# A banded attention with a gated MLP on one core: the same steps in another written-out order, on other PSUM banks

## The chip, the cores and the metric

One core of one Trainium2 chip runs the whole program. The metric is the time on the device in microseconds. The kernel before was run three times without a profile and once with one; every trace row below comes from the profiled run.

## The reference, cut to what matters

The input has 8 batches, 8 heads, 576 positions and a head size of 64. Heads 0 to 3 attend to the last 32 positions, heads 4 to 7 to the earlier positions that agree modulo 32. The heads' results side by side are `x` (8 x 576 tokens, 512 wide), and a gated MLP with a convolution over three neighbouring tokens follows.

```python
scores = np.where(masks, q @ k.T / sqrt(64), -1e9)
x = softmax(scores) @ v
h = np.maximum(x @ w_in, 0.0)                        # 512 -> 1024
conv_out = sum(conv_w[k] * h_shifted[k] for k in range(3))
out = (h * sigmoid(conv_out)) @ w_out                # 1024 -> 512
```

## The kernel before, in words

**Attention** works in 32 units, one for each batch and pair of heads. A unit loads q and k together (`load_qk`, L218) and v (`load_v`, L223) into one of two buffers, unit n into buffer n mod 2. TensorE makes the scores (L369, with masks at L376) in one half of the PSUM tile `r`. DVE and ACT make the softmax, and DVE transposes it into `tt` (L447). TensorE then makes the values from `tt` and v (L470). From unit 4 on, the values of unit n and the scores of unit n + 1 are one step, a "visit". ACT copies the values as rounded `xh` (L503), DVE takes the rest as `xl` (L528). So the load of q for unit n + 2 waits for the scores of unit n, and the load of v for unit n + 2 for the values of unit n.

**Weights** arrive as 64-bit floats in blocks of 512 KB (L245), and DVE, ACT, POOL (clamp, L281) and TensorE split each into a high and a low part, the `w_in` blocks first and then the `w_out` blocks (`convert`).

**The MLP** takes the 4608 tokens in 9 groups of 512. For each group `mm1` makes 8 blocks of 128 hidden channels: per block four product steps of three matmuls each (high by high, low by high, high by low; L567), gathered in one of four PSUM banks `m0` to `m3`. `conv_gate` then works on one block: ACT evicts it with relu (L580), ACT scales it (L592; DVE at L595 for some blocks of the first group), DVE adds the two neighbours (L601), ACT takes tanh (L604), DVE the gate (L605), ACT and POOL split the result into `gh` and `gl` (L608, L610). POOL also carries two tokens from group to group (L582, L584). `mm2` makes the 4 output blocks of a group, eight product steps each (L633), ACT evicts a block (L640) and SyncE stores it (L643).

The blocks in flight live in the tile `misc`: three buffers `h` and three buffers `c`, used in turn. `mm2` evicts its output blocks into the same buffers: three of the four into `c` buffers, which the next group's scale writes, and one into an `h` buffer, which the next relu writes. A later block can take such a buffer only when the store that reads it has landed.

**The order** is written out by hand. Each `op(...)` call appends one step with its engine, what it reads and what it writes, and gives it the next number (0 to 2148). `ORDER` (L42) lists all numbers, and the program is emitted in that order. Each engine has one queue and works through its steps in the order in which they were emitted. SyncE issues all 120 DMAs, loads and stores alike, in that way: a DMA whose buffer isn't free holds all that stand behind it. `BANKS` (L39) names the PSUM bank of each of the 128 accumulations. `FILLS` (L126) puts dummy products on a tile of zeros ahead of a step: a bank, a number of wide ones (512 columns) and of narrow ones (256).

```python
    def emit(self, busy):
        for i in ORDER:
            bank, wide, narrow = FILLS.get(i, (0, 0, 0))
            for j in range(wide + narrow):
                busy(bank, j < wide)
            self.ops[i][2]()
```

Steps that are named below:
- 30, 56, 69: the values of units 0, 2 and 3; 10, 22, 35, 48, 61: the scores of units 0 to 4; 317: the visit with unit 6's scores.
- 59 and 60: the loads of q and of v for unit 4; 47: the load of v for unit 3; 130 and 131: the last two blocks of `w_in`; 170 and 169: the first two blocks of `w_out`.
- 58: the `xl` of unit 2, which the scores of unit 4 need; 171: the clamp of the first `w_out` blocks, on DVE.
- 82, 92, 106, 115, 126, 128: TensorE's part in the splitting of `w_in` blocks.
- 1531, 1541, 1551, 1561: the four stores of group 5; 1699: the load of v for unit 29; 1569: the first scale that takes a buffer of step 1531.

Of the kernel before, what the change touches and what calls it, by code (L numbers as in the profile page):

```python
# [39 lines left out]
    "10321030203132021200031230013102313220230203213000233002203113020221123003211032002110233022132012030212233123121130032131002321"  # L40
)
ORDER = [  # L42
# [82 lines left out]
]  # L125
FILLS = {  # L126
    22: (0, 6, 1), 30: (0, 17, 1), 35: (1, 5, 1), 43: (0, 1, 1), 128: (0, 1, 1), 10: (0, 11, 0), 56: (4, 5, 0), 185: (4, 4, 1), 219: (2, 3, 0),
}

class Plan:  # L130
# [636 lines left out]
```

## Time and profile before

| What | us |
|---|---|
| median of 3 runs (lowest, highest) | 520.11 (519.94, 521.47) |
| the profiled execution's own time | 523.03 |
| its span in the profile | 521.0 |
| TensorE busy | 497.7 |
| DVE busy | 367.4 |
| ACT busy | 282.1 |
| POOL busy | 133.7 |

The span runs from the first to the last instruction of the profiled execution; its own time holds 2.0 us more around that. Busy time counts matmuls, loads of weights apart from them, and the work of the other engines; waiting and issuing of DMAs are not busy. Starts are counted from the beginning of the span. A wait is put down to what released it last.

### The profile page before, as it was taken

Reading aid. Unit: us, or ns where it says so; the run is one execution under the profiler, and the core shown is the slowest. Engines: PE = TensorE matmul, PEld = TensorE weight load, DVE = VectorE, ACT = ScalarE, POOL = GpSimd, SP = SyncE. Lnnn points to the kernel's source line nnn. Section 1 sums busy time; section 2 is a strip of 40 time slices with the busy share of each in tenths; the row PEclk is TensorE's granted clock in tenths of the full one; section 3 lists DMA queues with packets and bytes.
Section 4 is the critical chain, followed back from the end, with each engine's and each line's share of the span. In section 5 each row is a group of like instructions: output and inputs, shape, how many; then the busy total and the mean of one; then the engine's idle time right before and its main releaser. Section 6 shows DMA issues by size and latency. Waiting matters only on the chain.

```text
span 521.0 us, 15912 instructions
## 1 busy us (share of the span) xinstructions
PE 497.7 (96%) x6936; PEld 399.4 (77%) x6936; DVE 367.4 (71%) x655; ACT 282.1 (54%) x611; POOL 133.7 (26%) x216
## 2 busy tenths in 40 slices
PE   8778999999999999999998999999989999999997
PEld 4456768788888778878876888788768888878897
DVE  3996999786956797378767985798548855753640
ACT  4883687367624663257435743674347534755551
POOL 0200253023411251025302440233005220542240
PEclk9997999999999999999999999999989999999999
DMA  8583334432232304440252213422431202001001
GB/s 313 229 292 104 109 107 143 174 132 81 79 115 83 119 3 143 111 140 9 70 171 68 95 67 102 140 71 79 119 119 33 78 3 82 0 1 60 23 11 71
DMA packets 17349, 51.42 MB, mean 99 GB/s; under 512 B 2048, under 2 KB 2944, under 8 KB 17280
## 3 DMA queue, kind: packets, MB, share of 16 engines
q1 hardware_dynamic: 17280, 50.41, 28.5%
q8 instruction: 54, 0.88, 0.7%
q14 instruction: 15, 0.12, 0.1%
HBM read 40.97 MB, written 9.44 MB: 97 GB/s over the span
## 4 chain that ended last, share of the span: by engine, by line
PE 69%; DMA 6%; DVE 5%; ACT 4%; issue 1%; SPq 1%; ACTq 0%
PE m L633 37%; PE m L567 23%; DMA out_dram<-misc 6%; PE r L470 5%; PE r L369 3%; DVE misc L601 3%; ACT misc L592 1%; ACT misc L580 1%; DVE misc L605 1%; SPq L218 1%; DVE tt L447 1%; ACT misc L604 1%; ACT gh L608 1%; SPq L643 0%; ACT xh L503 0%
## 5 line engine op out<-in xcount | busy, mean ns | idle before, releaser
L601 DVE SCALAR_TENSOR_TENSOR misc<-misc,cw 128x512 f32<-128x512 f32 (+23 forms) x256 | 130.4, 548 | 48.2 <-ACT misc L592 46.6
L567 PE MATMUL m<-xh,wih 128*128 128x512 f32 x288 | 116.8, 406 | 4.3 <-ACT misc L580 4.3
L633 PE MATMUL m<-gh,woh 128*128 128x512 f32 (+2 forms) x320 | 119.5, 373 | 1.2 <-ACT misc L580 1.2
L633 PE MATMUL m<-gl,woh 128*128 128x512 f32 (+2 forms) x320 | 117.9, 369 | 0.0
L633 PE MATMUL m<-gh,wol 128*128 128x512 f32 (+2 forms) x320 | 117.8, 368 | 0.0
L610 POOL TENSOR_TENSOR gl<-misc,gh 128x512 fp32r<-128x512 f32 (+1 forms) x70 | 88.1, 1265 | 112.9 <-ACT gh L608 112.4
L567 PE MATMUL m<-xh,wil 128*128 128x512 f32 x288 | 113.9, 395 | 0.0
L567 PE MATMUL m<-xl,wih 128*128 128x512 f32 x288 | 113.7, 395 | 0.0
L592 ACT ACTIVATE misc<-misc,cw 128x255 f32<-128x255 f32 (+15 forms) x122 | 59.3, 523 | 22.6 <-DMA out_dram<-misc 12.3
L567 PEld LDWEIGHTS m<-xh,wih 128*128 128x128 f32 x288 | 55.1, 191 | 18.6 <-ACT misc L580 6.9
L633 PEld LDWEIGHTS m<-gh,woh 128*128 128x128 f32 x320 | 60.1, 188 | 12.0 <-ACT misc L580 1.7
L633 PEld LDWEIGHTS m<-gl,woh 128*128 128x128 f32 x320 | 60.1, 188 | 10.5 <-POOL gl L610 0.2
L604 ACT ACTIVATE misc<-misc 128x512 f32<-128x512 f32 (+1 forms) x72 | 44.8, 630 | 42.7 <-DVE misc L601 42.4
L633 PEld LDWEIGHTS m<-gh,wol 128*128 128x128 f32 x320 | 60.1, 188 | 9.7
L567 PEld LDWEIGHTS m<-xl,wih 128*128 128x128 f32 x288 | 55.1, 191 | 12.1
L567 PEld LDWEIGHTS m<-xh,wil 128*128 128x128 f32 x288 | 55.3, 192 | 10.8
L582 POOL COPY misc<-carry 128x2 f32<-128x2 f32 x64 | 21.3, 341 | 160.6 <-DMA out_dram<-misc 83.1
L580 ACT ACTIVATE misc<-m 128x512 f32<-128x512 f32 x72 | 42.7, 593 | 30.4 <-PE m L567 15.3
L605 DVE SCALAR_TENSOR_TENSOR misc<-misc 128x512 f32<-128x512 f32 (+1 forms) x72 | 51.0, 717 | 9.9 <-ACT misc L604 9.4
L608 ACT CAST gh<-misc 128x512 fp32r<-128x512 f32 (+1 forms) x72 | 43.9, 616 | 20.9 <-DVE misc L605 20.4
L640 ACT ACTIVATE misc<-m 128x512 f32<-128x512 f32 (+2 forms) x40 | 21.8, 558 | 46.1 <-PE m L633 45.9
L503 ACT CAST xh<-r 128x576 fp32r<-128x576 f32 (+13 forms) x56 | 23.8, 429 | 40.3 <-PE r L470 37.0
(76 smaller groups left out, 490.3 us busy)
## 6 DMA issues: line engine op xcount, KB each, us to landing
qk<-in_dram SPq DMA_DIRECT2D x32, 592.0 KB, 5.4
v<-in_dram SPq DMA_DIRECT2D x32, 384.0 KB, 4.0
ws<-in_dram SPq DMA_DIRECT2D x14, 512.0 KB, 4.8
out_dram<-misc SPq DMA_DIRECT2D x28, 256.0 KB, 4.1
misc<-in_dram SPq DMA_DIRECT2D x2, 512.0 KB, 8.4
out_dram<-misc SPq DMA_DIRECT2D x4, 255.5 KB, 2.8
out_dram<-misc SPq DMA_DIRECT2D x3, 256.5 KB, 2.1
more<-in_dram SPq DMA_DIRECT2D x1, 320.0 KB, 5.7
```

The costliest lines, as they stand in the source:

```text
L470: nc.tensor.matmul(psV[64 * h:64 * h + 64, o:o + n_], v[W * c:W * c + W, h, j], tt[W * c:W * c + W, 64 * NBLK * h + a:64 * NBLK * h + z], ...
L503: op(A, "xh", lambda hi=hi, src=src: nc.scalar.copy(hi, src), ko, [("xh", hp, x) for x in halves], n=z - a)
L567: nc.tensor.matmul(ps, a[:, n, fs], x[:, c, N * x0:N * x0 + N], start=(n == 0 and m == 0), stop=(n == NC - 1 and m == 2))
L580: op(A, "relu", lambda: nc.scalar.activation(out=h[:, 2:N + 2], in_=ps, func=AF.Relu), [kp], [("h", hi)], n=N)
L592: op(A, "scale", lambda a=a, z=z: nc.scalar.activation(out=c_[:, a:z], in_=h[:, a + 1:z + 1], func=AF.Copy, scale=w1), kh + ["cw"], (kc if ...
L601: op(V, "conv", lambda k=k, wk=wk, a=a, z=z: nc.vector.scalar_tensor_tensor(out=c_[:, a:z], in0=h[:, a + k:z + k], scalar=wk, in1=c_[:, a: ...
L604: op(A, "tanh", lambda: nc.scalar.activation(out=c_[:, :n], in_=c_[:, :n], func=AF.Tanh, scale=0.5), kc, kc, n=n)
L605: op(V, "gate", lambda: nc.vector.scalar_tensor_tensor(out=c_[:, :n], in0=c_[:, :n], scalar=1.0, in1=h[:, 1:n + 1], op0=ALU.add, op1=ALU.m ...
L608: op(A, "gh", lambda: nc.scalar.copy(row(gh, g, f)[:, :n], c_[:, :n]), kc, [(k, "h") for k in keys], n=n)
L610: op(es, "gl", lambda: se.tensor_tensor(out=row(gl, g, f)[:, :n], in0=c_[:, :n], in1=row(gh, g, f)[:, :n].bitcast(F32), op=ALU.subtract), ...
L633: nc.tensor.matmul(ps, a[:, f, ms], row(y, g, f)[:, tok], start=(f == 0 and n == 0), stop=(f == NF - 1 and n == 2))
L640: op(A, "out", lambda ps=ps, a0=a0, z=z: nc.scalar.activation(out=o[:, a0:z], in_=ps, func=AF.Copy, scale=0.5), [("M", mi)], ko, n=z - a0)
```

## The change

`BANKS`, `ORDER` and `FILLS` get new contents; nothing else is changed. The list has the same 2149 numbers, each once. The order differs on every engine: on TensorE's first 170 steps nearly all stand elsewhere, and SyncE's first nine DMAs alone keep their places without a break.

On SyncE, around the loads for unit 4, the order before was: 131, 34 (v of unit 2), 130, 170, 47, 169, 59 (q of unit 4), 299 and 315 (q of units 5 and 6), 60 (v of unit 4), 300. It is now: 131, 130, 59, 170, 169, 60, 47, 315, 300, 299, with 34 further ahead.

For group 5, before: 1510 (v of unit 28), 1699, 1561, 1715 (q of unit 30), 1541, 1551, 1531. Now: 1531, 1510, 1561, 1551, 1715, 1699, 1541.

The fillers, wide and narrow: values of unit 0 from 17 + 1 to 13 + 1; scores of unit 2 from 5 + 1 to none; step 92 from none to 6; step 115 from none to 4 + 1; values of unit 1 from 1 + 1 to none; step 128 from 1 + 1 to 2; values of unit 2 from 5 to 2; scores of unit 4 from none to 6; values of unit 3 from none to 2 + 1; steps 185 (4 + 1) and 219 (3) to none; visit 317 from none to 2. Scores of units 0 (11) and 1 (6 + 1) keep theirs.

The diff, cut to the two constants and the parts of the list that are spoken of:

```diff
 BANKS = (
-    "10321030203132021200031230013102313220230203213000233002203113020221123003211032002110233022132012030212233123121130032131002321"
+    "10322312121131300313023013133002101213101003123022131132231032011032302113023132013202133102103230210313023203022230113021332010"
 )
 ORDER = [
-    0, 19, 7, 20, 2, 1, 8, 3, 4, 18, 72, 74, 73, 9, 97, 117, 98, 118, 6, 10, 5, 11, 33, 12, 13, 22, 23, 46, 84, 21, 24, 14, 85, 75, 25, 15, 86, 16,
-    87, 76, 17, 99, 88, 77, 30, 100, 89, 78, 101, 31, 90, 92, 79, 108, 32, 109, 102, 93, 119, 26, 103, 27, 80, 28, 35, 104, 110, 91, 111, 81, 82, 36,
-    112, 94, 120, 113, 95, 96, 37, 114, 115, 38, 121, 105, 106, 131, 34, 122, 130, 29, 123, 39, 124, 43, 40, 83, 125, 44, 41, 128, 45, 126, 129, 132,
-    48, 127, 170, 47, 156, 49, 133, 169, 157, 59, 50, 42, 299, 221, 51, 134, 135, 116, 56, 52, 137, 143, 57, 53, 107, 144, 58, 54, 138, 61, 171, 222,
-    315, 62, 60, 172, 145, 55, 158, 136, 173, 223, 174, 182, 183, 63, 176, 64, 69, 177, 184, 70, 300, 65, 71, 185, 66, 67, 146, 186, 159, 68, 147,
-    139, 188, 149, 148, 195, 150, 160, 196, 140, 162, 161, 197, 151, 208, 141, 163, 152, 224, 175, 189, 198, 153, 178, 190, 199, 301, 154, 164, 155,
...
-    1503, 1539, 1560, 1548, 1507, 1530, 1508, 1549, 1504, 1562, 1550, 1505, 1630, 1540, 1506, 1511, 1596, 1520, 1699, 1561, 1563, 1512, 1715, 1541,
-    1597, 1551, 1513, 1531, 1631, 1521, 1598, 1514, 1564, 1601, 1584, 1515, 1565, 1516, 1599, 1566, 1579, 1570, 1569, 1580, 1600, 1571, 1581, 1604,
...
+    0, 19, 7, 20, 2, 1, 8, 3, 4, 18, 72, 74, 73, 9, 97, 98, 117, 5, 10, 11, 33, 118, 12, 13, 22, 6, 14, 23, 84, 15, 24, 16, 85, 25, 86, 87, 75, 17,
+    76, 89, 30, 88, 77, 26, 31, 34, 99, 27, 46, 78, 100, 21, 32, 79, 108, 90, 92, 109, 101, 28, 80, 110, 81, 82, 102, 35, 111, 83, 29, 103, 119, 36,
+    112, 120, 113, 37, 114, 115, 38, 104, 105, 106, 131, 121, 122, 143, 130, 59, 107, 39, 43, 124, 123, 91, 40, 125, 94, 44, 116, 128, 45, 41, 126,
+    129, 48, 127, 132, 170, 182, 169, 49, 95, 96, 144, 133, 50, 42, 156, 51, 134, 157, 135, 183, 93, 52, 56, 137, 57, 53, 60, 171, 47, 58, 172, 138,
+    61, 54, 173, 221, 315, 62, 158, 63, 222, 136, 55, 64, 174, 69, 223, 65, 70, 300, 299, 145, 71, 146, 66, 176, 159, 67, 147, 184, 148, 149, 160,
+    177, 139, 175, 185, 140, 162, 141, 150, 224, 186, 142, 195, 188, 151, 234, 209, 208, 189, 152, 235, 163, 196, 153, 273, 164, 154, 197, 190, 165,
...
+    1502, 1559, 1503, 1529, 1560, 1504, 1505, 1539, 1530, 1506, 1562, 1531, 1510, 1549, 1508, 1561, 1596, 1550, 1597, 1551, 1511, 1563, 1520, 1715,
+    1699, 1598, 1512, 1601, 1564, 1521, 1565, 1513, 1579, 1566, 1514, 1599, 1569, 1540, 1580, 1571, 1515, 1541, 1664, 1573, 1698, 1600, 1516, 1613,
...
 ]
 FILLS = {
-    22: (0, 6, 1), 30: (0, 17, 1), 35: (1, 5, 1), 43: (0, 1, 1), 128: (0, 1, 1), 10: (0, 11, 0), 56: (4, 5, 0), 185: (4, 4, 1), 219: (2, 3, 0),
+    22: (0, 6, 1), 30: (0, 13, 1), 10: (0, 11, 0), 56: (5, 2, 0), 92: (0, 6, 0), 128: (3, 2, 0), 69: (4, 2, 1), 115: (2, 4, 1), 61: (0, 6, 0),
+    317: (5, 2, 0),
 }
```

## Rows read from the trace of the kernel before

**Rows 1.** The page: span, and busy time of an engine with its share and instructions.

```profile
span 521.0 us, 15912 instructions
...
PE 497.7 (96%) x6936; PEld 399.4 (77%) x6936; DVE 367.4 (71%) x655; ACT 282.1 (54%) x611; POOL 133.7 (26%) x216
```

**Rows 2.** Waits of TensorE: who waited for whom; us in total, times, longest.

```profile
PE r L369 <- DMA qk<-in_dram: 4.4, 3, 1.9
PE m L567 <- ACT misc L580: 4.3, 5, 2.1
PE r L470 <- DVE tt L447: 3.2, 5, 1.4
PE r L369 <- issue: 1.6, 2, 1.2
...
PE m L633 <- ACT misc L580: 1.2, 1, 1.2
```

**Rows 3.** TensorE in order of time: start, us, what, xcount [wait before <-releaser].

```profile
9.94 3.95 PE L653 MATMUL m<-warm 128*128 128x512 bf16 x18
15.24 1.13 PE L470 MATMUL r<-tt,v 32*64 32x32 f32 x84 [1.35 <-DVE tt L447]
...
40.03 0.32 PE L369 MATMUL r<-qk 64*32 64x64 f32 x13 [1.94 <-DMA qk<-in_dram]
...
42.26 0.42 PE L369 MATMUL r<-qk 64*32 64x64 f32 x3 [1.24 <-issue]
...
72.55 1.03 PE L470 MATMUL r<-tt,v 32*64 32x2 f32 x80 [0.50 <-DVE tt L447]
```

**Rows 4.** Two stretches: busy us of each engine, granted clock (PEclk), DMA share, GB/s.

```profile
41.60:48.50 6.90, 6.24 (x17) 4.81 (x17) 5.71 (x7) 1.15 (x2) 0.00 (x0) 0.51 0.47 150
386.40:389.80 3.40, 3.32 (x8) 2.65 (x9) 3.40 (x10) 2.84 (x7) 0.00 (x0) 0.50 0.02 5
```

**Rows 5.** SyncE's queue, 26 to 43 us: DMAs issued (merged where alike).

```profile
26.10 5.09 SPq L245 DMA_DIRECT2D ws<-in_dram  x2
31.28 0.88 SPq L223 DMA_DIRECT2D v<-in_dram  x1
...
32.69 10.35 SPq L218 DMA_DIRECT2D qk<-in_dram  x3
```

**Rows 6.** DMA issues, us to landing: 32.6 to 33.0, 43.0 to 43.5, 4.0 to 4.5.

```profile
qk<-in_dram SPq DMA_DIRECT2D x1, 592.0 KB, 7.2
...
v<-in_dram SPq DMA_DIRECT2D x1, 384.0 KB, 5.4
...
v<-in_dram SPq DMA_DIRECT2D x1, 384.0 KB, 9.9
```

**Rows 7.** DVE in order of time, 37 to 40 us.

```profile
37.23 0.76 DVE L528 TENSOR_TENSOR xl<-r,xh 128x576 fp32r<-128x576 f32 x1 [0.46 <-ACT xh L503]
...
39.04 0.69 DVE L281 TENSOR_SCALAR ws<-ws 128x1024 f32<-128x1024 f32 x1
```

**Rows 8.** The chain that ended last: start, us, what.

```profile
433.25 17.95 PE m L567 x78
```

**Rows 9.** SyncE's queue, 374 to 379 us.

```profile
374.67 0.33 SPq L223 DMA_DIRECT2D v<-in_dram  x1
...
376.95 1.42 SPq L643 DMA_DIRECT2D out_dram<-misc  x3
```

**Rows 10.** ACT, then TensorE, in order of time, 374 to 390 us.

```profile
385.04 0.91 ACT L592 ACTIVATE misc<-misc,cw 128x127 f32<-128x127 f32 x2 [4.78 <-DMA out_dram<-misc]
...
386.48 0.80 PE L567 MATMUL m<-xh,wih 128*128 128x512 f32 x1 [2.10 <-ACT misc L580]
```

**Rows 11.** The stores (L643): who waited for them, and time to landing.

```profile
  ACT misc L592: 12.3, 8
  ACT misc L580: 5.1, 2
...
DMA to landing us min/median/max: 2.0/3.8/7.0
```

148 rows, old and new, of the table ORDER are left out of this document.

## The prediction, made before the change was run

> **What bounds the kernel now.** Read the page's busy rows first. TensorE is busy for 497.7 of 521.0 us, so 23.3 us are idle, and no other engine comes near it [rows 1]. The work that the change can't touch is therefore large: it removes no product. Read next the granted clock, because a busy TensorE may be a slow one. In two stretches the clock shown is 0.51 and 0.50 of full speed, that is the level of 1.2 GHz in place of 2.4; they last 6.9 and 3.4 us [rows 4], and half of each is lost: 3.4 + 1.7 = 5.1 us. The full-speed work is 497.7 - 5.1 = 492.6 us, and 521.0 - 492.6 = 28.4 us is all that any order could win, ramp and tail included.
>
> Then read TensorE's waits [rows 2] and look each one up in time [rows 3]. They come from two places that an order can move.
>
> First, unit 4's scores: 1.94 us until the load of its q and k has landed, then 1.24 us of "issue" among the same scores, and the clock falls in that stretch [rows 3, 4]. SyncE shows why the load is late. Its queue is in order, and step 59 (q of unit 4) stands behind two w_out loads and v of unit 3; it goes out at 32.69 and takes 7.2 us [rows 5, 6].
>
> Second, the output stores. A group's results are written into buffers that the next group's gate (relu, scale) takes over, so ACT waits for the store to land: 12.3 us in 8 waits at the scale, 5.1 us in 2 at the relu [rows 11]. Group 5 shows the chain. v of unit 29 holds SyncE until 374.67, the four stores behind it go out from then to 378.4 [rows 9], ACT waits 4.78 us and frees a PSUM bank late, TensorE waits 2.10 us, and the second fall of the clock follows [rows 10, 4]. TensorE's share of such chains is 4.3 + 1.2 us for a bank [rows 2], and the 3.2 us for a transpose less the 1.35 and 0.50 us before 75 us [rows 2, 3], 1.35: in all 6.85 us.
>
> **The change, part by part.** All 2149 steps stay, and so does the filler: 53 wide and 6 narrow dummy products become 54 and 4. A wide one is 3.95 / 18 = 0.22 us [rows 3], so the difference is under 0.1 us: nothing. I count distances below in TensorE work between two steps of the list: a product step is three matmuls of 17.95 / 78 = 0.23 us, so 0.69 us [rows 8].
>
> *q of unit 4 moves ahead of both w_out loads and of v of unit 3.* It now follows step 130, which went out at 26.10 [rows 5], so it goes at about 26.5 and, with the 7.2 us it took before, lands by 33.7. TensorE was free for it at 40.03 - 1.94 = 38.09. What is late next is DVE: the scores need unit 2's `xl`, which ended at 37.23 + 0.76 = 37.99, and in the new list a clamp of 0.69 us stands ahead of it [rows 7]. So the scores start at 38.7 and not 40.03: 1.3 us gained (bounds 0 and 1.94). The w_out loads lose nothing, for the first waits for its own buffer until 30.9 [rows 5]. The issue wait of 1.24 us isn't tied to the list: 0 gained (bounds 0 and 1.24).
>
> *The clock there.* The wait of 1.35 us before unit 0's values was followed by no fall; the 1.94 us, with 1.24 more right after, were [rows 3, 4]. With some 0.6 + 1.24 us left and six wide fillers put ahead of these scores, I take the fall as gone: 3.4 us gained (bounds 0 and 3.4).
>
> *Fillers ahead of unit 0's values go from 17 to 13 wide.* That wait grows from 1.35 to 1.35 + 4 x 0.22 = 2.2 us [rows 3], and DVE still sets when it ends, so no time is lost by itself. It is however as long as the 2.10 us with which the later fall came, so a new fall at 15 us is possible. I take 0 (bounds 0 and a loss of 3.4, the half of a fall as long as the first).
>
> *v of unit 3 moves behind v of unit 4*, whose buffer comes free only with unit 2's values. Before, it went out at 31.28 [rows 5]. Now it goes 0.4 us after unit 2's values end. Until unit 3's values TensorE has six fillers (1.3), the scores (1.1), three product steps (2.1) and 2.5 fillers (0.5): 5.0 us. v of unit 4 took 5.4 us as second of a pair [rows 6]; 0.4 + 5.4 - 5.0 = 0.8 us lost. Bounds: 0, and with the 9.9 us that v took in the crowded start [rows 6], 5.3.
>
> *The stores.* Of the 24 of groups 0 to 5, 17 stood behind a load whose buffer came free only after the result was there; in the new list 6 do. In group 5, from the point where SyncE is released to the first scale that takes a stored buffer there were nine product steps (6.2 us); now step 1531 goes out at once and some 10 us lie between. The smallest cover per group, before and after, counted so: group 0 3.4 and 4.1, 1 4.8 and 4.8, 2 4.8 and 5.5, 3 4.1 and 6.8, 4 4.1 and 5.5, 5 6.1 and 9.1 us. Smaller bursts also land sooner: a store takes 2.0 to 7.0 us, 3.8 in the median [rows 11]. At the median none of 4.8 or more waits. At 7.0 with 0.4 of issue, groups 1, 2 and 4 would hold ACT for 2.6 + 1.9 + 1.9 = 6.4 us, and before 17.4 us of ACT became 6.85 of TensorE, 0.4 for one: 2.5 us. I take the middle, 1.3 us left, so 6.85 - 1.3 = 5.5 gained, and the second fall of the clock, 1.7 (together bounds 0 and 8.6).
>
> The DMA fit of the Trainium skill (DMA: Bandwidth & Descriptors, "Anatomy of one DMA — SWDGE (gpsimd) path") speaks against this part: about 2.0 us fixed plus the bytes at 436 GB/s, an estimate of 2.6 us for a 256 KB store, by which no landing would reach past a cover, the store term would be 0 and the sum 519.1 us. It is a fit of another issuing path, and the trace's 3.8 and 7.0 us decide.
>
> *What else the list moves.* PSUM banks reused within 1.5 us: 25 before, 23 after; 0. The shortest way from one unit's scores to the next ones is 7.1 us in place of 7.7: 0.6 lost at most once, which I charge. Loads that lost cover (q of unit 24 from 25 to 7.5, q of 27 from 24 to 9, v of 14 from 29 to 9.5 us) still have more than 7.2. For waits that I can't see the nearest price is what six groups cost before, 6.85, so 1.15 for one; I charge two groups, 2.3 (bounds 0 and 6.85).
>
> **Sum.** 1.3 + 3.4 - 0.8 + 5.5 + 1.7 - 0.6 - 2.3 = 8.2 us. Against the profiled execution that is a span of 521.0 - 8.2 = 512.8, and a time of 523.03 - 8.2 = 514.8 with the 2.0 us around the span. The median of the three runs, 520.11, lies 2.9 under that execution, so I forecast 520.11 - 8.2 = **511.9 us**.
>
> **The rivals.**
> - *Everything goes.* The new order meets landings as they are: 1.94 + 1.24 + 3.4 + 6.85 + 1.7 = 15.1 us, 505.0 us. For it: all these waits hang on transfers. Against: DVE stands right behind the first. Chance 0.15.
> - *The clock stays.* Waits shorten but both falls, or two others, remain: 8.2 - 5.1 = 3.1 gained, 517.0 us. For it: the longer wait before unit 0's values. The Trainium skill (TensorE: Matmul & The Clock Gate, Part 1: The HAM clock gate) says that the moment of the change is run-variable. The trace has one profile and can't show that. Chance 0.15.
> - *The engines behind the stores hold.* When ACT waits less, DVE's chain and the banks are late instead, and the store term is 0: 1.3 + 3.4 - 0.8 - 0.6 - 2.3 = 1.0, 519.1 us, not to be told from no change. For it: after the store waits DVE's transposes held TensorE too [rows 2]. Chance 0.12.
> - *The queue only changes victims.* A transfer put behind a blocked load is v of unit 3 now. If it lands as late as 9.9 us [rows 6], TensorE waits 5.3 us at about 40 us and the clock falls again (3.4), against 1.3 + 3.4 from unit 4; stores behind v of 17, q of 22 and v of 29 would then be as late as before, so their term is 0: 520.11 + 5.3 + 3.4 - 4.7 = 524.1 us. It decides once that load takes over 4.6 us, and ends slower from about 7.5 us, where wait and fall outweigh the 4.7 by more than 1.6. Against: by then the crowd of the start is over. Chance 0.11.
>
> That the change doesn't do what it says isn't open: the lists hold the same steps, and the queue positions above are read from them.
>
> **How the numbers follow.** The forecast (508 to 516) has 0.47. A measurement of this kernel tells about 0.3%, 1.6 us: faster is under 518.5, slower over 521.7. Faster: 0.47 + 0.15 + 0.15 = 0.77; slower 0.11; the rest, 0.12, the same. The range leaves out the better half of "everything" and most of "slower": 505.5 to 520.5.
>
> **What would show it.** Right: q of unit 4 issued before 27 us, the wait for q at unit 4 under 1 us, clock 1.00 from 40 to 50 us, ACT waiting under 4 us in all for stores, TensorE waiting under 2 us for a bank, a busy TensorE of about 493 us. Wrong: a wait for v before unit 3's values, a granted clock near 0.5 anywhere after 10 us, or waits of TensorE for DVE's transposes that grow as those for ACT shrink.

## The result, and the profile after

The changed kernel took 503.12 us in the median of four runs (502.82 to 503.48). The kernel before took 520.79 us (519.94 to 523.96; four runs, three of them those that the prediction knew). The ratio is 0.965, with a 95% interval from 0.961 to 0.969: 17.7 us less. That is faster than the forecast of 511.9, faster than the fast end of the range, and 1.9 us beyond the rival that let everything go. One execution of an experiment below, a tenth run of e1, took 2666.41 us and is left out there.

The page of the changed kernel, its span and busy row, as in [rows 1]. Line numbers after the constants are higher by one than before.

```profile
span 501.6 us, 15936 instructions
...
PE 491.8 (98%) x6935; PEld 396.9 (79%) x6935; DVE 368.5 (73%) x655; ACT 283.4 (57%) x611; POOL 132.8 (26%) x216
```

The profiled execution's own time is 503.48. Its span is 19.4 us shorter than the one of [rows 1]. TensorE's idle time went from 23.3 to 9.8 us, which is 13.5 of it; its busy time went from 497.7 to 491.8, which is 5.9. To see where, each span is cut at 95 us, by when the last weights have landed (at 94.2 us in the kernel before). The columns are the busy us of each engine, the granted clock, the DMA share and GB/s. The first pair is the kernel before, the second the changed one.

```profile
0.00:95.00 95.00, 83.46 (x1467) 57.78 (x1468) 78.69 (x130) 64.36 (x172) 20.50 (x35) 0.96 0.54 193
95.00:521.00 426.00, 414.24 (x5471) 341.64 (x5469) 288.76 (x526) 217.73 (x439) 113.18 (x181) 1.00 0.24 78
```

```profile
0.00:95.00 95.00, 89.02 (x1495) 61.59 (x1496) 84.63 (x139) 65.47 (x173) 22.63 (x33) 0.98 0.59 204
95.00:501.60 406.60, 402.81 (x5442) 335.35 (x5440) 283.88 (x518) 217.94 (x438) 110.20 (x183) 1.00 0.24 79
```

Idle time of TensorE is the length of a stretch less its busy time: 11.5 and 11.8 us before, 6.0 and 3.8 us after. So 5.6 us of idle time went in the first stretch and 8.0 in the second. The long quiet part, where the prediction followed one chain in detail, holds the larger share.

What still holds TensorE in the changed kernel (who waited for whom; us in total, times, longest), against [rows 2]:

```profile
PE r L471 <- ACT wih L287: 2.6, 1, 2.6
PE m L654 <- DVE warm L657: 1.1, 1, 1.1
PE r L471 <- ACT t L405: 0.9, 2, 0.7
PE m L311 <- DVE wl L296: 0.6, 1, 0.6
PE m L317 <- DVE wl L296: 0.3, 1, 0.3
PE r L370 <- DMA qk<-in_dram: 0.2, 1, 0.2
```

Both waits for ACT on a bank (4.3 and 1.2 us in [rows 2]) are gone, so is "issue" (1.6), and of the 4.4 us for q and k 0.2 is left. The last wait in this list ends at 71.2 us. The places that the prediction named, in order of time on TensorE:

```profile
15.19 1.32 PE L471 MATMUL r<-tt,v 32*64 32x32 f32 x84 [2.58 <-ACT wih L287]
...
37.72 1.47 PE L654 MATMUL m<-warm 128*128 128x512 bf16 x6
39.32 0.35 PE L370 MATMUL r<-qk 64*32 64x64 f32 x16
...
43.41 1.03 PE L471 MATMUL r<-tt,v 32*64 32x2 f32 x80
```

Unit 4's scores start at 39.32 without a wait, and unit 3's values at 43.41 too. Six dummy products (1.47 us) run ahead of those scores: they take most of the place of the old wait of 1.94 us, and the scores start only 0.7 us earlier than at 40.03 [rows 3]. The one wait that grew is the one before unit 0's values, from 1.35 [rows 3] to 2.58. The clock in the two stretches of [rows 4], and in the one that is slow now (same columns as the windows above):

```profile
41.60:48.50 6.90, 6.90 (x107) 5.33 (x106) 6.81 (x11) 4.46 (x9) 0.18 (x1) 1.00 0.75 256
15.80:19.30 3.50, 3.50 (x55) 1.97 (x41) 3.47 (x8) 2.76 (x7) 0.64 (x1) 0.51 0.93 323
386.40:389.80 3.40, 3.40 (x160) 2.75 (x158) 2.11 (x4) 1.50 (x4) 0.86 (x3) 1.00 0.02 5
```

SyncE's queue in the two places of [rows 5] and [rows 9]:

```profile
26.94 0.38 SPq L219 DMA_DIRECT2D qk<-in_dram  x1
...
355.91 0.34 SPq L644 DMA_DIRECT2D out_dram<-misc  x1
...
356.82 2.24 SPq L644 DMA_DIRECT2D out_dram<-misc  x2
...
365.25 0.34 SPq L644 DMA_DIRECT2D out_dram<-misc  x1
```

q of unit 4 goes out at 26.94 and lands at 33.73; it was 32.69 and 39.89. The four stores of group 5 no longer leave in one burst behind a blocked load. Who waits for the stores, and how long they take, against [rows 11]:

```profile
  ACT misc L581: 1.8, 2
  ACT misc L593: 1.4, 2
...
DMA to landing us min/median/max: 1.7/2.6/6.1
```

ACT waits 3.2 us for stores where it waited 17.4, and the median landing fell from 3.8 to 2.6 us. The fit of the Trainium skill named in the prediction (DMA: Bandwidth & Descriptors, "Anatomy of one DMA — SWDGE (gpsimd) path") gave an estimate of 2.6 us for such a store: this trace agrees in the median, the one before did not, and the longest, 6.1 us, is still far above it.

### The profile page after: what moved, and what is told of

Same layout as the page of the kernel before. It is cut to its first block, busy times and chain, and to the rows that moved or that the text cites. A ratio compares the mean times of both kernels' runs of the same rounds, so it can differ in the third digit from the quotient of the medians.

```text
span 501.6 us, 15936 instructions
## 1 busy us (share of the span) xinstructions
PE 491.8 (98%) x6935; PEld 396.9 (79%) x6935; DVE 368.5 (73%) x655; ACT 283.4 (57%) x611; POOL 132.8 (26%) x216
## 4 chain that ended last, share of the span: by engine, by line
PE 86%; DVE 7%; ACT 4%; issue 1%; POOL 1%; DVEq 0%; ACTq 0%
PE m L634 38%; PE m L568 36%; PE r L471 5%; PE r L370 4%; DVE misc L602 2%; PE m L654 2%; ACT t L405 1%; ACT t L446 1%; DVE ws L285 1%; ACT wa L283 1%; DVE misc L606 1%; DVE mx L392 1%; DVE wl L296 0%; DVE misc L596 0%; DVE sm L421 0%
## 5 line engine op out<-in xcount | busy, mean ns | idle before, releaser
L602 DVE SCALAR_TENSOR_TENSOR misc<-misc,cw 128x512 f32<-128x512 f32 (+26 forms) x256 | 131.2, 545 | 35.4 <-ACT misc L593 32.5
L611 POOL TENSOR_TENSOR gl<-misc,gh 128x512 fp32r<-128x512 f32 (+1 forms) x70 | 86.1, 1234 | 107.9 <-ACT gh L609 104.1
L568 PE MATMUL m<-xh,wih 128*128 128x512 f32 x288 | 113.9, 395 | 0.0
L568 PE MATMUL m<-xh,wil 128*128 128x512 f32 x288 | 112.3, 390 | 0.0
L568 PE MATMUL m<-xl,wih 128*128 128x512 f32 x288 | 112.3, 390 | 0.0
L593 ACT ACTIVATE misc<-misc,cw 128x383 f32<-128x383 f32 (+15 forms) x122 | 59.7, 523 | 8.2 <-POOL gl L611 4.2
L568 PEld LDWEIGHTS m<-xl,wih 128*128 128x128 f32 x288 | 54.1, 188 | 11.9 <-DVE xl L529 0.4
L568 PEld LDWEIGHTS m<-xh,wih 128*128 128x128 f32 x288 | 54.0, 188 | 11.8 <-ACT xh L504 0.2
L568 PEld LDWEIGHTS m<-xh,wil 128*128 128x128 f32 x288 | 54.1, 188 | 10.5
```

The costliest lines, as they stand in the source:

```text
L568: nc.tensor.matmul(ps, a[:, n, fs], x[:, c, N * x0:N * x0 + N], start=(n == 0 and m == 0), stop=(n == NC - 1 and m == 2))
L593: op(A, "scale", lambda a=a, z=z: nc.scalar.activation(out=c_[:, a:z], in_=h[:, a + 1:z + 1], func=AF.Copy, scale=w1), kh + ["cw"], (kc if ...
L602: op(V, "conv", lambda k=k, wk=wk, a=a, z=z: nc.vector.scalar_tensor_tensor(out=c_[:, a:z], in0=h[:, a + k:z + k], scalar=wk, in1=c_[:, a: ...
L611: op(es, "gl", lambda: se.tensor_tensor(out=row(gl, g, f)[:, :n], in0=c_[:, :n], in1=row(gh, g, f)[:, :n].bitcast(F32), op=ALU.subtract), ...
```

## The experiments

Two theories stood against each other. The first: the time is won by SyncE's queue places (the stores, and q of unit 4), and the new computing order only makes room for them. The rival: the computing order, its banks and fillers win it, and the queue places are incidental. Then single terms were measured. In the kernels of the experiments line numbers are 12 lower than before: L555 is a product of `mm1`, L621 one of `mm2`, L458 the values, L357 the scores, L568 the relu, L580 the scale. Times stand beside runs of the kernel before on the same chip, whose medians were 520.13 (e1 to e4), 520.41 (e5 to e8) and 521.51 (the second run of e1, e8b, e9 and e10). The changed kernel was not run again beside them: a difference to its 503.12 us is one between sessions, in which the medians of the kernel before differ by up to 1.4 us.

**e1, the early part alone.** The new list as far as it has the same steps done, then the old one.

```diff
-ORDER, BANKS, FILLS of the kernel before
+first 387 entries from the new ORDER, the rest in the old order; banks and fillers likewise
```

> The new list for its first 387 steps (to about 97 us), the old list, banks and fillers for the rest. Counted step by step, the lag of TensorE behind its full-speed work is 6.4 us smaller in the changed kernel by that point. If the gain is a sum of two separate parts, this kernel gains 6.4 us: 520.8 - 6.4 = 514.4 us (513 to 516). The rival, that the early gain is taken back by later waits on the same engines, gives 518 to 521.

Measured: 518.07 us in the median of nine runs (516.55 to 521.22), ratio 0.9959 [0.993, 0.9988], 2.1 us gained. Its profile comes from a second run of the same kernel:

> The same list as in e1_early (new for 387 steps, old after), for its profile. If the 6.4 us of the early part are there at 95 us and lost later, the lag of TensorE at 100 us is about 11 us and grows by more than the 7.9 us by which it grew after that point before. If they are not there, the lag at 100 us is 15 us or more, with a fall of the clock or waits for issue in the first 100 us.

That execution took 517.38 us with a span of 515.6. By 95 us TensorE has no wait over 0.8 us but the 1.05 us at its start and 2.35 us before unit 0's values, as in the changed kernel. Behind it the old list's waits are all back (TensorE in order of time):

```profile
380.75 0.50 PE L555 MATMUL m<-xh,wih 128*128 128x512 f32 x1 [1.69 <-ACT misc L568]
387.43 1.11 PE L458 MATMUL r<-tt,v 32*64 32x32 f32 x84 [1.54 <-DVE tt L435]
```

So starting ahead doesn't help the later chains: a store is late there for its place in the queue, not for the time of day. Nor is the lead taken back: it is 5.1 us for the product at 172.44 us (177.53 before) and 5.4 at the end of the two profiles. But 2.6 us of it are the clock (0.995 of full speed here, 0.990 in the profile before), in which typical runs of the two hardly differ (2.5 us lost over these nine, 2.6 over the 13 of the kernel before beside them). The early part is worth 2.1 us by e1, and 17.7 - 13.7 = 4.0 by e2 below, not the 6.4 that was expected.

**e2, the late part alone.** The old list to its 452nd entry, then the new one.

```diff
-ORDER, BANKS, FILLS of the kernel before
+first 452 entries in the old order, the rest from the new ORDER; banks and fillers likewise
```

> The old list for its first 452 steps (to about 110 us), the new list, banks and fillers for the rest. The lag shrinks by a further 13 us after that point in the changed kernel, all of it between groups 1 and 5. If the parts add: 520.8 - 13 = 507.8 us (506 to 510), with the fall of the clock at 41.6 us still there and none after. The rival, that the later part pays only after an earlier start, gives 513 or more.

Measured: 506.48 us (505.99 to 508.53), ratio 0.9723 [0.9676, 0.977], 13.7 us gained. With the 2.1 of e1 that is 15.8 of 17.7: the two parts nearly add, and three quarters come from the late one. The early waits stay as they were:

```profile
39.32 0.32 PE L357 MATMUL r<-qk 64*32 64x64 f32 x13 [1.82 <-DMA qk<-in_dram]
...
40.99 0.30 PE L357 MATMUL r<-qk 64*32 64x64 f32 x3 [0.67 <-issue]
```

No fall of the clock followed these two, though the same list had one behind 1.94 and 1.24 us [rows 3, 4]. The only slow stretch was at 16.2 to 19.6 us. It followed a wait of 1.37 us before unit 0's values, and the same list had none behind 1.35 us there [rows 3].

**e3, SyncE's order alone.** Computing order, banks and fillers as before; SyncE's 120 DMAs in the new order.

```diff
-SyncE: ... 131, 34, 130, 170, 47, 169, 59, 299, ...
+SyncE: ... 34, 46, 21, 131, 130, 59, 170, 169, 60, 47, ...
-SyncE, group 5: 1510, 1699, 1561, 1715, 1541, 1551, 1531
+SyncE, group 5: 1531, 1510, 1561, 1551, 1715, 1699, 1541
```

> The old order on TensorE, DVE, ACT and POOL, the old banks and fillers; only SyncE's queue has the new order. Theory 1 (the places in SyncE's queue are the cause): stores go out when their results are there, ACT's waits for stores fall from 17 us below 5, q of unit 4 is issued before 28 us, and at least 10 of the 17.7 us are gained: 503 to 511 us. Theory 2 (the order on the computing engines is the cause, since it sets when buffers are taken again): less than 5 us, 516 to 521 us.

Measured: 515.05 us (513.33 to 516.18), ratio 0.9869 [0.9812, 0.9926]: 5.1 us gained, between the two theories. ACT's waits for stores fell from 17.4 to 8.3 us. But other waits stayed or grew. Two of TensorE's largest, and above them one of POOL:

```profile
63.86 1.30 POOL L269 TENSOR_SCALAR ws<-ws 128x1024 f32<-128x1024 f32 x1 [3.51 <-DMA ws<-in_dram]
...
70.52 1.56 PE L458 MATMUL r<-tt,v 32*64 32x2 f32 x80 [3.14 <-DVE tt L435]
...
370.98 0.44 PE L458 MATMUL r<-tt,v 32*64 32x48 f32 x22 [1.26 <-issue]
```

At 70.52 stands the visit with unit 6's scores: a wait of 0.50 us in [rows 3], now 3.14, with the clock at 0.50 from 70.2 to 77.0 us. It is put down to DVE's transpose, but DVE had itself waited 1.95 us for ACT, ACT 2.86 us for POOL's clamp, and POOL 3.51 us for a `w_out` block. So a load is late here too. In the changed kernel, whose SyncE order is the same, this visit has no wait: the new computing order is what removes it.

**e4, the computing order without the stores' places.** The changed kernel, with 14 stores of groups 0 to 5 put back behind loads that stood ahead of them before.

```diff
-SyncE, group 5: 1531, 1510, 1561, 1551, 1715, 1699, 1541, 1698
+SyncE, group 5: 1510, 1715, 1699, 1531, 1698, 1541, 1551, 1561
```

> The changed kernel, with 14 stores of groups 0 to 5 put behind those loads in SyncE's queue behind which they stood before; the order on the computing engines, the banks and the fillers stay new. Theory 1: ACT waits for stores again (over 10 us), and 5 to 13 us are lost: 508 to 516 us, with a wait of TensorE for a bank in most groups. Theory 2: the new order takes the buffers later or has other work for TensorE, so at most 3 us are lost: 503 to 506 us.

Measured: 530.31 us (529.43 to 531.33), ratio 1.0173 [1.0127, 1.0219]. It is 27 us slower than the changed kernel and slower than the kernel before. One chain of several, first SyncE, then ACT, then TensorE in order of time, and the stretch around it (busy us of each engine, granted clock):

```profile
108.68 1.38 SPq L211 DMA_DIRECT2D v<-in_dram  x1
110.16 0.37 SPq L631 DMA_DIRECT2D out_dram<-misc  x1
...
115.08 1.09 ACT L568 ACTIVATE misc<-m 128x512 f32<-128x512 f32 x2 [8.06 <-DMA out_dram<-misc]
...
115.73 0.80 PE L303 MATMUL m<-woh,negr 128*128 128x512 f32 x1 [6.43 <-ACT misc L568]
```

```profile
112.70:119.50 6.80, 3.77 (x9) 3.00 (x10) 2.59 (x4) 2.87 (x6) 1.73 (x7) 0.50 0.18 68
```

The store leaves behind v at 110.16; ACT has waited 8.06 us when its relu can write, and TensorE 6.43. Two more such waits of 4.54 and 5.16 us follow at 224 and 285 us, each with the clock at 0.50 or 0.51 for 6.8 or 6.9 us. ACT waits 28.0 us for stores in all. So the rival falls in its strong form: with late stores the new computing order loses. How much it would lose with SyncE's old queue is not shown, for that was not run. The loads keep their new order here, and seven of the 14 stores stand also behind loads that stood behind them before; the store at 110.16 is one, now behind q of units 10 and 11. Together with e3 it says that order and queue places bring most of what they bring together.

**e5, q of unit 4 late again.**

```diff
-SyncE: 131, 130, 59, 170, 169, 60, 47, 315
+SyncE: 131, 130, 170, 47, 169, 59, 60, 315
```

> The changed kernel, with q of unit 4 behind both w_out loads and v of unit 3 in SyncE's queue, as it stood before, and v of unit 3 ahead of v of unit 4. By my first term the scores of unit 4 then wait for q again by 1.3 to 2 us and the clock may fall: 1.3 to 5 us slower, 504.4 to 508 us. The rival, that DVE's work for the next units sets the pace there and hides the wait: within 1 us of 503.1.

Measured: 504.58 us (504.25 to 504.84), ratio 0.9711 [0.9682, 0.9739], 1.5 us slower than the changed kernel, which is about as much as the sessions differ. One row of DVE and one of TensorE:

```profile
39.70 0.69 DVE L269 TENSOR_SCALAR ws<-ws 128x1024 f32<-128x1024 f32 x1 [2.83 <-DMA ws<-in_dram]
...
41.11 0.35 PE L357 MATMUL r<-qk 64*32 64x64 f32 x16 [2.88 <-DVE xl L516]
```

The wait is 2.88 us long and no fall of the clock followed it. It is not put down to q, which landed at 40.62, but to unit 2's `xl`, which ended at 41.05: DVE had waited 2.83 us for a `w_out` block that this edit puts behind v of unit 3, and only then came the clamp and `xl`. So the edit made two loads late, and it does not measure the price of q alone, 1.3 us. The 3.4 us for the clock did not hang on this wait.

**e6, more fillers before unit 0's values**, so that the wait of 2.58 us is covered.

```diff
-30: (0, 13, 1)
+30: (0, 23, 1)
```

> The changed kernel, with 23 in place of 13 wide fillers ahead of unit 0's values, which fill the 2.58 us wait before them. If that wait is why the clock falls at 15.8 us, the fall goes and up to 1.7 us are gained: 501.4 to 502.8 us. The rival, that DVE's splitting of the weights sets the pace up to 30 us, or that the fall comes from what TensorE did earlier: 502.8 to 503.5 us, or a fall all the same.

Measured: 504.85 us (504.17 to 506.19). That is slower than either figure expected. The clock stayed at 1.0 throughout the profiled execution and TensorE is 0.9 us ahead at 59 us (the expectation of e9 says 1.2), but it lost that again:

```profile
67.67 0.30 PE L458 MATMUL r<-tt,v 32*64 32x32 f32 x3 [1.61 <-issue]
```

An issue wait, in a kernel of which only the number of fillers at 10 us differs. The next run asks what it is.

**e7, the issue waits.** The kernel before; at step 10 eleven wide fillers become twenty-two narrow ones. The columns are the same, TensorE's list is 11 matmuls longer from there on.

```diff
-10: (0, 11, 0)
+10: (0, 0, 22)
```

> The kernel before, with the 11 wide fillers ahead of the first scores cut into 22 narrow ones of the same columns: 22 more instructions on TensorE at the start, the same work. If the issue waits are the fetch of the next block of instructions (16 KB at a time on the instruction queue) and fall where TensorE's list crosses into a block, they move by 11 matmuls towards the front: the one at 261 us comes before the last 33 of the visit's matmuls and not the last 22, the one at 42 us before the last 14 and not the last 3. The rival, that they come from crowded transfers or at random: they stay at the same matmuls or appear in other steps. The time changes by less than 2 us either way.

Measured: 521.46 us (518.44 to 524.29, ten runs), ratio 1.0024 [0.999, 1.0059], no difference that this measurement can tell. First one issue wait of the kernel before, then the same in e7:

```profile
261.15 0.44 PE L470 MATMUL r<-tt,v 32*64 32x64 f32 x22 [0.78 <-issue]
```

```profile
40.80 0.38 PE L357 MATMUL r<-qk 64*32 64x64 f32 x14 [1.44 <-issue]
...
258.73 0.54 PE L458 MATMUL r<-tt,v 32*64 32x64 f32 x33 [1.51 <-issue]
```

In the same two steps 14 matmuls are left behind the wait where there were 3 [rows 3], and 33 where there were 22: 11 more each time. The wait sits at a place in TensorE's list, whatever step stands there. The count of matmuls up to that place, the first (x...) of each row, says the same (the windows from the start to just ahead of the waits at 42.26 us before, at 40.80 us in e7, at 67.67 us in e6 and at 69.59 us in e10, below; the last three show TensorE alone):

```profile
0.00:42.25 42.25, 32.07 (x732) 18.46 (x733) 29.72 (x52) 31.69 (x104) 5.91 (x16) 0.99 0.72 264
```

```profile
0.00:40.79 40.79, 32.69 (x732) 1.00 0.75 273
```

```profile
0.00:67.66 67.66, 62.39 (x1242) 1.00 0.62 217
```

```profile
0.00:69.58 69.58, 62.55 (x1242) 0.98 0.63 211
```

All issue waits of all these kernels stand behind matmul 350, 732, 1242, 1878, 3921, 4303, 5704 or 6342, to within one. The distances are multiples of about 127.5 matmuls, each with its load of weights, so 255 instructions, and the page of each kernel lists 54 packets of instructions on one of its queues, 0.88 MB together, so 16 KB each, while TensorE has 54 such stretches. The reading is that the engine waits there for the next piece of its program, and the trace has the times of these packets. Of the 27 issue waits of TensorE over 0.15 us in all these kernels, 26 end 1.2 to 1.5 us after such a packet has landed, and one 0.7 us after. For the wait that ends at 42.26 us, for one, the packet moved from 39.97 to 40.94. All but those at 1878 fell in score and value steps, whose matmuls are short: 80 take 1.03 us [rows 3]. Not every border in such a step costs something. In the changed kernel every packet had landed at least 1.3 us before TensorE came to its border. Why some packets are late and others not is not settled here.

**e10, the same shift in the changed kernel**, ten wide fillers at step 10 as twenty narrow ones.

```diff
-10: (0, 11, 0)
+10: (0, 1, 20)
```

> The changed kernel, with 10 of the 11 wide fillers ahead of the first scores cut into 20 narrow ones: the same columns, 20 more instructions on TensorE. If the place of the block borders in the list is worth what e6_more_fill showed, the issue waits of 1.6 and 0.5 us at 68 and 111 us come back and the kernel takes 504 to 506 us. The rival, that those waits came with that run: no issue wait over 0.3 us, 502.5 to 503.5 us.

Measured: 506.08 us (504.76 to 506.36), ratio 0.9709 [0.9668, 0.9751], 3.0 us more than the changed kernel. The issue waits came as expected:

```profile
69.59 0.30 PE L458 MATMUL r<-tt,v 32*64 32x32 f32 x3 [1.47 <-issue]
113.23 0.39 PE L621 MATMUL m<-gl,woh 128*128 128x512 f32 x1 [0.56 <-issue]
```

Nothing else was changed. From profile to profile e10 loses 2.7 us: TensorE is 0.8 us behind by 37 us, ahead of any issue wait, and 1.6 to 1.8 us go around the three issue waits (0.32 us at 41.30 us is the third). So where these borders fall is worth less than 2 us here.

**e8 and e8b, the old fillers in the new order.** e8 keeps the counts of the kernel before, on banks that are free there; in e8b, whose edit is shown, the four that waited for ACT themselves (steps 43 and 128) are left out.

```diff
-22: (0, 6, 1), 30: (0, 13, 1), 10: (0, 11, 0), 56: (5, 2, 0), 92: (0, 6, 0), 128: (3, 2, 0), 69: (4, 2, 1), 115: (2, 4, 1), 61: (0, 6, 0), 317: (5, 2, 0),
+22: (0, 6, 1), 30: (0, 17, 1), 35: (2, 5, 1), 10: (0, 11, 0), 56: (0, 5, 0), 185: (4, 4, 1), 219: (2, 3, 0),
```

> The changed kernel, with the fillers of the kernel before (on banks that are free). If the moved fillers hold the clock around unit 4 and cover late landings, they are worth 1 to 4 us: 504 to 507 us. If fillers only fill waits that others set: within 1 us of 503.1 us.

> As e8_old_fill, without the four fillers that themselves waited there for a PSUM bank (ahead of unit 1's values and of step 128). If the 6 us of e8_old_fill came from those waits: within 1.5 us of 503.1. If the fillers ahead of unit 4 and of the w_in steps are what the new list needs: 505 us or more again, with waits of 1.3 us or more and a fall of the clock between 35 and 70 us.

Measured: e8 509.45 us (506.96 to 511.51), ratio 0.9803 [0.9759, 0.9846]; e8b 507.82 us (507.24 to 510.16), ratio 0.9759 [0.9708, 0.981]. e8 is slower than its expectation allowed. e8b has three wide fillers less than the changed kernel and takes 4.7 us more. Two of its waits, both without a counterpart in the changed kernel:

```profile
39.66 0.35 PE L357 MATMUL r<-qk 64*32 64x64 f32 x16 [1.53 <-DVE xl L516]
...
62.20 0.50 PE L303 MATMUL m<-woh,negr 128*128 128x512 f32 x1 [1.84 <-DVE wol L306]
```

The first stands where the changed kernel has six fillers of 1.47 us, so it is no loss by itself. The old ones at steps 35, 185 and 219 (twelve wide and two narrow, 13 x 0.22 = 2.9 us) run ahead of steps that may have been ready. The number of fillers hardly differs, so it is their places that cost; which of them cost how much was not taken apart.

**e9, an attempt to beat the changed kernel.** 23 wide fillers before unit 0's values, as in e6, and ten taken out at steps 92 and 115, so that everything behind keeps its place in TensorE's list.

```diff
-30: (0, 13, 1), 92: (0, 6, 0), 115: (2, 4, 1)
+30: (0, 23, 1), 115: (2, 0, 1)
```

> The changed kernel, with ten fillers moved: ahead of unit 0's values 23 in place of 13, ahead of steps 92 and 115 none and 0 + 1 in place of 6 and 4 + 1. From there on every instruction of TensorE keeps its place in the blocks that are fetched. In the run with the ten fillers added the clock did not fall, TensorE was 1.2 us ahead at 59 us, and 1.6 us of an issue wait then took that back. If block places are the reason, this kernel keeps the gain: 501.5 to 502.5 us, and no issue wait. If the filler removed was needed: 503 to 505 us.

Measured: 502.85 us (501.51 to 503.71, six runs), ratio 0.9651 [0.9617, 0.9685], the same as the changed kernel within what can be told. Its profile has the clock whole:

```profile
core 0: 500.7 us, clock 0.999
```

The issue wait of e6 at 67.67 us is not in it, as it should be. The fall at 16 us is gone too: the six runs list clocks of 0.999 to 1.000, the four of the changed kernel 0.995 to 0.997. That brought 0.9 us of span and 0.3 us in the median, where half of its 3.5 us, 1.7, was at stake. TensorE leads the changed kernel by 1.4 to 1.6 us from 37 to 325 us and loses 0.6 of it by the end, a part of it in an issue wait that the expectation did not allow for:

```profile
359.11 0.45 PE L458 MATMUL r<-tt,v 32*64 32x46 f32 x25 [0.28 <-issue]
```

It stands at the border of matmul 5704, where the changed kernel, with the same list from 36 us on, has no wait.

## Why the prediction was wrong, point by point

The direction was right, and the two waits that the prediction named did go; the size was wrong: 8.2 us forecast, 17.7 measured. The steps that failed: 5.0 us were charged for waits not seen, and none came; two terms were put at nothing, the issue waits (3.0 us of TensorE's waiting) and the places of the fillers (4.7 us); and the clock was priced 4.4 us too high. These figures overlap and don't add up to the difference. The signs of being right all came; of the signs of being wrong one came, a clock near 0.5 after 10 us, at 15.8 us.

- **q of unit 4** (1.3 us): right in its queue. Issued at 26.94 (26.5 forecast) and landed at 33.73 (33.7), with DVE's clamp and `xl` next to be late, as forecast. The scores started at 39.32, not at 38.7. What the load is worth alone was not measured, for e5 made a second load late.
- **Store waits** (5.5 us): right in kind, small in size. All of the 6.85 us went, for TensorE has no wait for a bank left. The 1.3 us that I kept back for late landings never came: smaller bursts also land sooner (2.6 us in the median, not 3.8). Its working left out group 0, whose cover of 4.1 us was the shortest, and group 3; with them it would have kept back 2.1 us, still further off. e4 shows how much the new order hangs on this term: 27 us, with stores that in part are later than they were in the old one. The prediction's price, taken from the old order, could not see that.
- **Charges for waits not seen** (0.8 for v of unit 3, 0.6 for the visits, 2.3 for the rest; 5.0 us with the 1.3 above): none came. v of unit 3 landed at 42.88, before the values at 43.41. After 71.2 us TensorE has no wait of 0.15 us or more. I priced what I could not see by what the old list had lost, and the new list lost nothing of the kind.
- **"The issue wait isn't tied to the list: 0 gained"**: the step that failed in its reasoning. e7 and e10 show that these waits are tied to the list, by the count of matmuls ahead. The kernel before has five of them, 0.33 + 1.24 + 0.78 + 0.53 + 0.16 = 3.0 us; the changed kernel has none, and e10, in which three come back, loses 1.6 to 1.8 us around them. A place in the list does not settle it alone: e7 has 5.1 us of such waits in its profile and takes no longer than the kernel before that can be told.
- **Fillers: "nothing"**: failed as well. Their number hardly changed, but their places are worth 4.7 us (e8b). The one filler term that I did follow, the wait before unit 0's values growing to 2.2 us with a possible fall of the clock, came true: 2.58 us, and a slow stretch of 3.5 us. That the longer wait made the stretch is not shown by the change: e2 has one there behind 1.37 us, with the old fillers. That it hangs on the wait is, by e9, where wait and stretch are gone.
- **Clock** (3.4 + 1.7 us): both falls are gone from the profile, and for a typical run I should not have counted them. 37 later runs of the kernel before list mean clocks between 0.990 and 1.000; (1 - clock) x span averages 2.6 us over them, and 1.9 over the four runs of the changed kernel. The profiled execution had 0.990, the low end. So the clock gave 0.7 us between typical runs, where I carried 5.1 over from one profile to the median. The errors hid each other, which was luck: without the clock the forecast was 3.1 us, and 17.0 were measured.

The ledger from profile to profile: of the 19.4 us, 1.9 are the wait for q of unit 4, 6.9 the chain of the stores, 3.0 the issue waits and 3.4 the clock (5.1 less 1.7). Another 2.2 are the waits for q of units 1 and 2 (1.39 and 1.07, now 0.24), which I had left aside though [rows 2] hold them in the 4.4; the first was 0.19 in e7, whose list is the old one, and in e2, whose early list is the old one too, neither is over 0.1, so they vary by run and are not the change's. The wait before unit 0's values took 1.2 back. That makes 16.2. The other 3.2 lie in short waits for DVE and ACT before 80 us and in restarts: the kernel before has 26 waits of over 0.15 us, the changed one 7, and a product behind a wait shows 0.50 us where one in a run shows 0.39. I did not measure these apart.

Of the rivals, "everything goes" (505.0 us) came nearest, and had 0.15. It was held back by "DVE stands right behind the first"; DVE did stand there, and the new list puts six fillers into that time. "The queue only changes victims" did not happen: v of unit 3 took its place behind v of unit 4 and met no one. That queue places can decide the sign shows in e4, with the stores and not with v. "The engines behind the stores hold" did not come: the one long wait for DVE, in e3 at 70.52 us, goes back to a load, and the stores begin only at 92 us.

Open is how the late gain divides. With SyncE's order alone (e3) TensorE's waits behind 80 us are 2.2 us for issue (0.68, 0.30, 1.26) and 2.0 us for ACT (1.20, 0.80). What else the new computing order wins there over the old one was not taken apart, nor what the new banks give by themselves.

## What to carry to other kernels

Price a new order as one thing: the queue places alone gave 5 us, the computing order with 14 stores behind loads lost 10, both together won 18, so a sum over these separate edits would not have found it. Count, in the emitted list of the busiest engine, which instruction stands at a place where it has been seen to wait for "issue", and try whether the time falls when such places are moved out of steps made of short instructions: it rose by 3 us with them in e10, and hardly moved in e7. Take terms that vary from run to run, the clock above all, from all runs listed and not from the one that was profiled.

## What the hardware showed that was not expected

- Waits for "issue" on TensorE belong to fixed counts of its instructions (matmul 732, 1242 and 5704 in kernels whose order differs), 0.16 to 1.61 us each, and move by exactly as many matmuls as are added ahead. 26 of 27 end 1.2 to 1.5 us after a 16 KB packet of instructions has landed.
- A wait does not decide by its length whether the granted clock falls: 2.88 us (e5) and 1.82 with 0.67 us (e2) had no fall behind them, 2.10 us [rows 10] and 2.58 us had, and before unit 0's values 1.35 us had none and 1.37 us (e2) had one. The Trainium skill (TensorE: Matmul & The Clock Gate, Part 1: The HAM clock gate) says of the start of a kernel that the moment of the change varies from run to run. These traces agree beyond the start: the same program's clock lies between 0.990 and 1.000 in 37 runs. The three runs at 0.990 took 522.7 to 523.9 us, the three at 1.000 518.5 to 519.5.
- Stores that leave alone land sooner. In the kernel before, the 7 of 34 that left with no other transfer in flight took 2.1 us in the median, the 12 that left with three or more in flight 5.8. In the changed kernel these are 13 and 3, and the median of all fell from 3.8 to 2.6 us.
